# Running sums in one early transfer, zeros on TensorE, and quarters of the first expert layer ahead of time

## The chip, the cores and the metric

The kernel runs on one core of a Trainium2 chip. Its five engines each work through a queue of their own: TensorE (PE; its weight loads are PEld) multiplies, VectorE (DVE) and ScalarE (ACT) work element by element and read the products, GpSimd (POOL) helps on data outside the product buffers, and SyncE (SP) issues transfers. The metric is the device time of one execution in microseconds (us).

## What is computed

Attention with a running-sum bias, then a dense mixture of four experts, then a two-layer network with squared relu, all in float32:

```python
scores = scale * np.matmul(q, k.transpose(0, 1, 3, 2))      # q, k: (2, 8, 576, 64)
cum = np.cumsum(np.maximum(s, 0.0), axis=-1)                # s: (2, 8, 576)
bias = -(cum[:, :, :, None] - cum[:, :, None, :])
scores = np.where(causal, -1e9, scores + np.minimum(bias, 0.0))
attn = softmax(scores)                                      # denominator + 1e-9
x = (attn @ v) as rows of 512                               # 1152 rows
p = domain_probs / (domain_probs.sum(-1, keepdims=True) + 1e-09)
out = sum over e of p[:, e:e+1] * (np.maximum(x @ w1[e], 0) @ w2[e])   # 512 -> 1024 -> 512
r = np.maximum(out @ w_in, 0)                               # 512 -> 2048
return (r * r) @ w_out
```

## The kernel before, in words

Every exact product is made of float32r parts: an operand is split into a rounded high part and the rest (`less`, line 76), and three products (high by high, high by low, low by high) are summed in a product buffer.

**Steps.** Attention runs as a pipeline over steps, one step for one tile of queries of one head (loop at line 683). Steps 0 to 15 are batch 0, queries 0 to 255, eight heads with two tiles each, two heads to a loaded group. Steps 16 to 39 are batch 0, queries 256 to 575, eight heads with three tiles. From step 40 on comes batch 1. In iteration n, step n gets its scores on TensorE (`do_qk`, line 415), step n-1 its masked scores and row minimum on VectorE (`do_scores`, the reduction, line 459), step n-2 its exponentials on ScalarE (`do_exp`, line 473), step n-3 its sums and scaling (VectorE, lines 485 and 486, and GpSimd, line 489), step n-4 its transposes on TensorE (line 512), and step n-5 their copy out (line 536). Two heads' attention times v (`do_pv`, line 560) gives a 128-row slice of x, which `do_x` (line 577) splits into `xh` and `xl`.

**Running sums.** The raw s is loaded eight times into 128 rows (`sc`, line 590), made positive and scaled on VectorE (line 593), and summed by a scan (line 594). For steps 0 to 15 the sums enter the scores as matmuls with a one-hot operand `pick` (line 610, made from `one`, line 608, a copy of parts of the identity), with the parts `cum_k` and its negation `cum_q`. For all later steps the sums of all 576 columns, split in two parts (`aug`, lines 626 to 628), are written to memory (`aug_d`, line 630) and read back as rows of the operands `th` and `tl`, whose other rows come from q and k. All this stands ahead of the loop in the code; so do the loads of the first four groups' q and k (`raw_p`, line 323) and of the expert shares (`praw`, line 623). `p_norm` (line 632) turns `praw` into shares with four VectorE operations at n = 12 in the code.

**Weights.** The first expert's sixteen weight pieces are loaded (`w_load`, line 91, three buffers) and split (`w_split`, ScalarE line 114 and VectorE line 78) at the steps of `SPLIT_AT`: the eight of the first layer at steps 0 to 14, the eight of the second at 22 to 36.

**Fill.** The first expert's work on tokens 0 to 255 is cut into parts (`fill_of`, line 663): eight column blocks of the first layer (`first`: 12 matmuls of 256 columns, line 196, over four 128-row slices of x, each from one pair of heads), then the second layer (`second`, line 222). They are issued between steps 21 and 45 at an even rate of columns per step (`X_AT`, line 31), those of tokens 256 to 511 after step 45. The experts that follow (lines 763 to 1111) have an order of their own.

**Order.** SyncE's queue keeps the order of the code. The other engines' order is made by a scheduler that goes by modelled times; `issue_after` puts instructions behind a given one on its engine, `pin` and `manual_schedule` keep the code's order.

Of the kernel before, what the change touches and what calls it, by code (L numbers as in the profile page):

```python
# [16 lines left out]
P = 128  # L17
# [11 lines left out]
SPLIT_AT = [*range(0, 16, 2), *range(22, 38, 2)]  # L29
NP = 5  # L30
X_AT = 21, 45
KMAX = 512

# [13 lines left out]
def fused_kernel(ctx, tc, qk, v, s, dp, w1, w2, wi, wo, out):  # L47
# [17 lines left out]
    make_identity(nc, ident)  # L65
# [4 lines left out]
    aug_d = dram.tile([2, B * H, 2, S], F32, name="aug_d")  # L70
# [119 lines left out]
    def l1_pe(e, c, f):  # L190
        t0, n = c
        ps = ph_tile()
        i = 0
        for kk in range(KD):
            for wh, x in ((0, xh), (0, xl), (1, xh)):
                nc.tensor.matmul(  # L196
                    ps[:, :n],
                    lhsT=w1_ap(e, wh, kk, f),
                    rhs=x[:, kk, t0 : t0 + n],
                    start=(i == 0),  # L200
                    stop=(i == 3 * KD - 1),
                )
                i += 1
        return ps
# [95 lines left out]
    with tc.tile_pool(name="att", bufs=2) as att, tc.tile_pool(name="atc", bufs=1) as const_a:  # L300
# [15 lines left out]
        st_pools[:] = [att, WBUF, "raw_w"]
# [18 lines left out]
        def bc_load(g):  # L335
            if g.plain:
                return
            r0 = g.b * H + g.heads[0]
            nc.sync.dma_start(out=g.th[AQ, : g.nq].bitcast(F32), in_=aug_d[0, r0, :, g.q0 : g.q1])
            nc.sync.dma_start(out=g.tl[AK, S : S + g.nk].bitcast(F32), in_=aug_d[1, r0, :, : g.nk])  # L340

        def part(name):
            tiles = [const_a.tile([P, 2 * S], F32R, name=f"{name}{i}") for i in range(2)]
            for t in tiles:
                c, ones = (slice(0, S), AK) if name == "th" else (slice(S, 2 * S), AQ)
                nc.gpsimd.memset(t[:64, c].bitcast(F32), 0.0)
                nc.gpsimd.memset(t[ones, c].bitcast(F32), 1.0)
            return tiles

        th_tiles, tl_tiles = part("th"), part("tl")  # L350
        for i, g in enumerate(groups):
            g.th, g.tl = th_tiles[i % 2], tl_tiles[i % 2]
# [62 lines left out]
        def do_qk(t):  # L415
            u, g = t.u, t.u.group
            if g.plain:
# [9 lines left out]
                one = pick[rows, u.h // 2, :]  # L427
                sums = ((one[:, : t.n], cum_k[rows, : t.w]), (cum_q[rows, t.q0 : t.q0 + t.n], one[:, : t.w]))
                for i, (lhs, rhs) in enumerate(sums):
                    nc.tensor.matmul(ps[: t.n, : t.w], lhsT=lhs, rhs=rhs, start=False, stop=(i == 1))  # L430
# [18 lines left out]
        def do_scores(t):  # L449
# [22 lines left out]
        def do_exp(t):  # L472
            nc.scalar.activation(  # L473
# [130 lines left out]
        pick = wt[0, 2, 3][:, 0, :].rearrange("p (h n) -> p h n", n=256)  # L604
# [4 lines left out]
        for a, z in ((0, 1), (1, 4)):  # L609
            nc.scalar.copy(pick[:, a:z, :], one[:, a:z].unsqueeze(2).to_broadcast([P, z - a, 256]))  # L610
        sums_to(P, 0, 256, 0.0)
        cum_k = att.tile([P, 256], F32R, tag="cum_k", name="cum_k", bufs=1)
        cum_q = att.tile([P, 256], F32R, tag="cum_q", name="cum_q", bufs=1)
        nc.scalar.copy(cum_k, cum[:, :256])
        for r0 in (32, 96):
            rows = slice(r0, r0 + 32)
            less(nc.vector, cum_k[rows], cum[rows, :256], cum_k[rows])
        nc.vector.tensor_scalar(cum_q, cum_k.bitcast(F32), -1.0, None, op0=ALU.mult)
        sums_to(B * H, 256, S, cum[: B * H, 255:256])
        cum = cum[: B * H, :]  # L620
        augs = [att.tile([B * H, 2, S], F32R, tag="ptk", name="aug", bufs=3) for _ in range(2)]
# [41 lines left out]
        def fill_of(c):  # L663
            tiles = range(c[0] // P, (c[0] + c[1]) // P)

            def first(f):
                l1_evac(0, c, f, l1_pe(0, c, f))
# [6 lines left out]
            parts = [(lambda f=f: first(f), 12 * c[1]) for f in range(NF)]  # L674
            return parts + [(lambda t=t, f=f: second(t, f), 3 * DM) for t in tiles for f in range(NF)]

# [6 lines left out]
        for n in range(nsteps + 8):  # L683
# [476 lines left out]
```

## Time and profile before

| | us |
|---|---|
| median of 3 runs | 718.39 (718.21 to 718.71) |
| the profiled execution | 719.2 |
| its span, first to last instruction | 717.4 |
| busy: TensorE, VectorE, ScalarE, GpSimd | 689.6, 507.6, 353.1, 311.9 |
| TensorE busy in the first 10 us, the next 10 | 2.15, 7.75 |

"Busy" counts the time in which an engine has at least one instruction under way; a matmul's end is modelled, so a TensorE that is marked busy need not run at its peak. A timeline row tells when an instruction began, how long it took, its engine, line, operation and tile, and in brackets how long the engine had been idle and for whom it waited. On SyncE a row is the issue of a transfer, not the transfer.

### The profile page before, as it was taken

What the parts mean: (1) busy time and instruction counts of PE and PEld (TensorE: products, weight loads), DVE (VectorE), ACT (ScalarE), POOL (GpSimd) and SP (SyncE); (2) the same over time, 40 slices, a digit from 0 to 9 for tenths busy, and PEclk for the clock granted to TensorE, in tenths of its full rate; (3) what the DMA queues carried; (4) which work ended last, traced back from release to release, by engine and by line L of the source; (5) the groups of instructions that cost most, each with busy time, mean ns of one, the idle gap of its engine ahead of it and who ended that gap; (6) DMA issues with size and microseconds to landing.
All of it is one profiled execution on the core that took longest, in us unless ns stands there. A gap on an engine that the chain in (4) does not pass through costs nothing.

```text
span 717.4 us, 11852 instructions
## 1 busy us (share of the span) xinstructions
PE 689.6 (96%) x4100; PEld 598.5 (83%) x4100; DVE 507.6 (71%) x1145; ACT 353.1 (49%) x881; POOL 311.9 (43%) x332
## 2 busy tenths in 40 slices
PE   4999999999999999999999999999999999999997
PEld 3678788778998998989989989889997888899996
DVE  6668667762378548787787787869587788955463
ACT  4789767752254453443342534335474445535341
POOL 4446534431043675292580852822528625704000
PEclk9999999999999999999999999999999999999999
DMA  4554333200121234344242443441203232210012
GB/s 139 169 162 148 93 85 84 62 25 1 60 84 64 89 114 136 108 136 139 85 165 90 148 147 105 132 121 70 60 22 111 77 122 96 89 30 1 1 59 73
DMA packets 37179, 66.37 MB, mean 93 GB/s; under 512 B 4512, under 2 KB 12208, under 8 KB 37120
## 3 DMA queue, kind: packets, MB, share of 16 engines
q1 hardware_dynamic: 27904, 40.45, 18.7%
q10 hardware_dynamic: 9216, 25.17, 10.7%
q8 instruction: 32, 0.52, 0.3%
q14 instruction: 27, 0.22, 0.1%
HBM read 52.87 MB, written 10.90 MB: 89 GB/s over the span
## 4 chain that ended last, share of the span: by engine, by line
PE 74%; DVE 12%; ACT 4%; issue 4%; DMA 2%; POOL 2%; SPq 1%; ACTq 0%; DVEq 0%; POOLq 0%
PE y L953 26%; PE ph L935 17%; PE pc L935 7%; PE ph L196 7%; PE y L222 6%; PE o L560 4%; PE pt L512 3%; DVE dy L144 2%; PE s L439 2%; DVE raw_d L148 2%; PE s L440 1%; DVE raw_d L140 1%; ACT p L473 1%; POOL w L78 1%; DVE h L988 1%
## 5 line engine op out<-in xcount | busy, mean ns | idle before, releaser
L953 PE MATMUL y<-w,h 128*128 128x512 f32 x1080 | 276.7, 393 | 0.7 <-ACT h L993 0.7
L953 PEld LDWEIGHTS y<-w,h 128*128 128x128 f32 x1080 | 194.2, 188 | 32.0 <-ACT h L993 0.9
L935 PE MATMUL ph<-tx,w 128*128 128x256 f32 (+1 forms) x720 | 116.2, 297 | 0.1
L935 PEld LDWEIGHTS ph<-tx,w 128*128 128x128 f32 x720 | 106.9, 190 | 7.6 <-ACT u L976 0.9
L976 ACT COPY u<-ph 128x256 f32<-128x256 f32 (+1 forms) x120 | 47.7, 397 | 96.1 <-PE ph L935 93.9
L78 POOL TENSOR_TENSOR w<-raw_w,w 128x512 fp32r<-128x512 f32 x58 | 79.4, 1383 | 21.5 <-ACT w L902 21.5
L935 PE MATMUL pc<-xh,w 128*128 128x256 f32 (+1 forms) x320 | 78.2, 299 | 6.2 <-DVE r L992 2.8
L935 PE MATMUL ph<-xh,w 128*128 128x256 f32 (+1 forms) x320 | 78.3, 299 | 1.7 <-DVE h L988 1.2
L489 POOL TENSOR_SCALAR p<-p,stat 128x128 f32<-128x128 f32 (+8 forms) x80 | 46.8, 597 | 72.8 <-DVE stat L486 30.4
L78 POOL TENSOR_TENSOR w<-val,w 128x512 fp32r<-128x512 f32 x40 | 58.6, 1480 | 43.4 <-PE ph L196 41.7
L133 POOL TENSOR_SCALAR dy<-dy 128x512 f32<-128x512 f32 x32 | 20.0, 626 | 116.1 <-ACT dy L131 108.7
L935 PEld LDWEIGHTS pc<-xh,w 128*128 128x128 f32 x320 | 55.9, 188 | 10.4 <-DVE h L988 3.8
L935 PEld LDWEIGHTS ph<-xh,w 128*128 128x128 f32 x320 | 56.1, 189 | 5.1 <-DVE h L988 1.9
L473 ACT ACTIVATE p<-p,stat 128x128 f32<-128x128 f32 (+8 forms) x80 | 46.6, 583 | 23.7 <-DVE stat L459 20.3
L222 PE MATMUL y<-w,h 128*128 128x512 f32 x216 | 57.7, 396 | 0.0
L196 PE MATMUL ph<-xh,w 128*128 128x256 f32 (+1 forms) x256 | 57.3, 299 | 0.1
L459 DVE CUSTOM_DVE_ANT_0 p<-s,mask 128x128 f32<-128x128 f32 (+8 forms) x80 | 35.8, 451 | 17.7 <-PE pt L512 8.8
L935 PE MATMUL ph<-xl,w 128*128 128x256 f32 (+1 forms) x160 | 47.5, 297 | 0.0
L935 PE MATMUL pc<-xl,w 128*128 128x256 f32 (+1 forms) x160 | 47.3, 296 | 0.0
L994 DVE TENSOR_TENSOR h<-r,h 128x256 fp32r<-128x256 f32 (+1 forms) x64 | 36.2, 571 | 13.7 <-ACT h L993 12.5
L196 PEld LDWEIGHTS ph<-xh,w 128*128 128x128 f32 x256 | 43.1, 188 | 1.5 <-DVE h L210 0.4
L222 PEld LDWEIGHTS y<-w,h 128*128 128x128 f32 x216 | 38.7, 188 | 6.2 <-DVE stat L459 0.3
(135 smaller groups left out, 1272.7 us busy)
## 6 DMA issues: line engine op xcount, KB each, us to landing
raw_w<-in_w SPq DMA_DIRECT2D x64, 256.0 KB
raw_d<-in_wi ACTq DMA_DIRECT2D x16, 512.0 KB
staged<-dy ACTq DMA_DIRECT2D x32, 256.0 KB
raw_d<-in_wo ACTq DMA_DIRECT2D x16, 512.0 KB
raw_w<-staged SPq DMA_DIRECT2D x32, 256.0 KB
raw<-in_qk SPq DMA_DIRECT2D x40, 144.0 KB
v<-in_v SPq DMA_DIRECT2D x8, 256.0 KB
out<-acc_a SPq DMA_DIRECT2D x6, 256.0 KB
```

The source lines that it names most:

```text
L78: eng.tensor_tensor(out_, a, b.bitcast(F32), op=ALU.subtract)
L196: nc.tensor.matmul(ps[:, :n], lhsT=w1_ap(e, wh, kk, f), rhs=x[:, kk, t0 : t0 + n], start=(i == 0), stop=(i == 3 * KD - 1),)
L222: mm = nc.tensor.matmul(ps, lhsT=h[:, hh, o : o + P], rhs=w2_ap(e, wh, f), start=(f == 0 and i == 0), stop=(f == NF - 1 and i == 2),)
L459: nc.vector.tensor_tensor_reduce(t.p[: t.n, a:z], ps[: t.n, : z - a], t.bias[:, a:z], scale=-0.125, scalar=init, op0=ALU.add, op1=ALU.min, ...
L473: nc.scalar.activation(t.p[: t.n, : t.w], t.p[: t.n, : t.w], AF.Exp, bias=t.nmax, scale=-1.0, accum_out=t.st[: t.n, 4 + t.c : 5 + t.c],)
L489: nc.gpsimd.tensor_scalar(t.p[: t.n, : t.w], t.p[: t.n, : t.w], t.st[: t.n, 6 + t.c : 7 + t.c], 1.0, op0=ALU.mult, op1=ALU.mult)
L512: nc.tensor.transpose(tp_ap(t, j), t.p[: t.n, kt[j] : kt[j + 1]], ident[: t.n, : t.n])
L560: return nc.tensor.matmul(u.o[i * D : (i + 1) * D, qs - u.q0 : u.nq], lhsT=vv[:kn, j, i * D : (i + 1) * D], rhs=rhs, start=(j == 0), stop= ...
L935: nc.tensor.matmul(ps[:, :n], lhsT=pw[q][s][:, wh, c : c + P], rhs=x_part(b, xn, xx, k2), start=(first and m == 0), stop=(m == 5), skip_gr ...
L953: nc.tensor.matmul(ps, lhsT=hs[j][:, hh, o : o + P], rhs=wt[e, 2, g][:, wh, j * DM : (j + 1) * DM], start=(g % 2 == 0 and i == 0 and j == ...
L976: nc.scalar.copy(t[:, :n], ps[:, :n])
L994: nc.vector.tensor_tensor(lo, r, hi.bitcast(F32), op=ALU.subtract)
```

## The change

- s comes in one transfer of its first 256 columns into all 128 rows, issued first, and one of the other 320 columns into 16 rows. Relu and factor are made on ScalarE. The high and low parts of the sums are made by a cast and one operation with a per-row factor `is_low` into `less_cum`; there are two one-hot operands, plus and minus, in place of a negated sum.
- The sums of columns 256 to 575, their split and their write (once, not twice with the sign turned) move to step 4 (`AUG_AT`, `later_sums`). The sign goes into the constant rows of `tl`.
- `p_norm`, the later sums and the weight splits get places behind step n-1's reduction; the splits also behind step n-2's exponentials. The first-layer splits start at step 2, not 0.
- TensorE multiplies a tile of zeros by itself: nine matmuls of 512 columns at the start, and one behind the scores of each of the steps 0 to 8.
- For tokens 0 to 255 and column blocks 0 to 3, the first layer's products of a 128-row slice of x are issued one quarter per step after that slice's pair of heads is done (pairs 0 to 2), into two product buffers that hold two blocks each; what is left in the fill for these blocks is the last slice.

```diff
-SPLIT_AT = [*range(0, 16, 2), *range(22, 38, 2)]
+SPLIT_AT = [*range(2, 17, 2), *range(22, 38, 2)]
+WARM = 9, 1, 9
+AUG_AT = 4
...
-    def l1_pe(e, c, f):
+    def l1_pe(e, c, f, ps=None, kks=range(KD), start=True):
         t0, n = c
-        ps = ph_tile()
-        i = 0
-        for kk in range(KD):
+        ps = ph_tile() if ps is None else ps
+        i = 3 * kks[0]
+        for kk in kks:
...
+        zeros = const_a.tile([P, 512], F32R, name="zeros")
+        nc.vector.memset(zeros.bitcast(F32), 0.0)
+
+        def keep_warm(after, n):
+            with tc.issue_after(after) if after is not None else nullcontext():
+                for _ in range(n):
+                    nc.tensor.matmul(idle, lhsT=zeros[:, :P], rhs=zeros, start=True, stop=True)
+
+        idle = ph_tile()
+        keep_warm(None, WARM[0])
...
-        for r0 in range(0, P, B * H):
-            nc.sync.dma_start(out=sc[r0 : r0 + B * H, :], in_=s)
+        nc.sync.dma_start(
+            out=sc[:, :256],
+            in_=s[:, :256].unsqueeze(0).to_broadcast([P // (B * H), B * H, 256]),
+        )
...
-            nc.vector.tensor_scalar(sc[:rows, c0:c1], sc[:rows, c0:c1], 0.0, 8.0, op0=ALU.max, op1=ALU.mult)
+            nc.scalar.activation(sc[:rows, c0:c1], sc[:rows, c0:c1], AF.Relu, scale=8.0)
...
+                nc.sync.dma_start(out=sc[: B * H, 256:], in_=s[:, 256:])
...
+        def pick(i, a, z):
+            src = one[:, a:z].unsqueeze(2).to_broadcast([P, z - a, 256])
+            nc.scalar.activation(picks[i][:, a:z, :], src, AF.Copy, scale=1.0 - 2.0 * i)
...
+        nc.vector.tensor_copy(high, cum[:, :256])
+        nc.vector.scalar_tensor_tensor(
+            less_cum, high.bitcast(F32), is_low, cum[:, :256], op0=ALU.mult, op1=ALU.subtract
+        )
...
+        def later_sums():
+            sums_to(B * H, 256, S, cum[: B * H, 255:256])
+            parts = att.tile([B * H, 2, S], F32R, tag="raw", name="aug", bufs=3)
+            total = cum[: B * H, :]
+            nc.scalar.copy(parts[:, 0, :], total)
+            less(nc.vector, parts[:, 1, :], total, parts[:, 0, :])
+            nc.sync.dma_start(out=aug_d, in_=parts.bitcast(F32))
...
             def first(f):
-                l1_evac(0, c, f, l1_pe(0, c, f))
+                if c[0] == 0 and f < 4:
+                    l1_evac(0, c, f, l1_pe(0, c, f, halves[f], range(KD - 1, KD)))
+                else:
+                    l1_evac(0, c, f, l1_pe(0, c, f))
...
+        def begin(kk):
+            if kk == 0:
+                for f in (0, 2):
+                    ps = ph_tile()
+                    halves[f], halves[f + 1] = ps[:, :256], ps[:, 256:]
+            early.extend(lambda f=f: quarter(kk, f) for f in range(4))
...
                 do_qk(cur)
+                if n < WARM[2]:
+                    keep_warm(cur.mm.ins, WARM[1])
+                if early:
+                    with tc.issue_after(cur.mm.ins):
+                        early.pop(0)()
...
             if n in SPLIT_AT:
-                w_step()
+                with tc.issue_after(s1.red.ins), tc.issue_after(s2.exp.ins):
+                    w_step()
+            if n == AUG_AT:
+                with tc.issue_after(s1.red.ins):
+                    later_sums()
             if n == 12:
-                p_norm()
+                with tc.issue_after(s1.red.ins):
+                    p_norm()
```

TensorE's queue at the program's start held the scores of steps 0 to 2 (raw_p is q and k, cum_k and cum_q the running sums):

```order
L420 MATMUL s<-raw_p 128x128
L420 MATMUL s<-raw_p 128x256
L420 MATMUL s<-raw_p 128x128
L430 MATMUL s<-cum_k,w 128x128
L430 MATMUL s<-cum_k,w 128x256
L430 MATMUL s<-cum_k,w 128x128
```

In the changed program it begins with the zeros (L332), and one more follows each step's sums (less_cum):

```order
L332 MATMUL ph<-zeros 128x512 x9
L436 MATMUL s<-raw_p 128x128
L436 MATMUL s<-raw_p 128x256
L436 MATMUL s<-raw_p 128x128
L449 MATMUL s<-less_cum,w 128x128
L449 MATMUL s<-w,less_cum 128x128
L332 MATMUL ph<-zeros 128x512
L449 MATMUL s<-less_cum,w 128x256
L449 MATMUL s<-w,less_cum 128x256
L332 MATMUL ph<-zeros 128x512
```

The scores of q and k keep their place, and the zeros have come in ahead of and between them.

VectorE's queue from the first scan to step 2's reduction held, before, the sums of all columns, their parts, and the first operation of `p_norm` (L634); L459 is the reduction:

```order
L594 SCALAR_TENSOR_TENSOR cum<-sc 128x256
L594 SCALAR_TENSOR_TENSOR cum<-sc,cum 16x320
L78 TENSOR_TENSOR cum_k<-cum,cum_k 32x256 x2
L618 TENSOR_SCALAR cum_q<-cum_k 128x256
L78 TENSOR_TENSOR aug<-cum,aug 16x576
L628 TENSOR_SCALAR aug<-aug 16x1152
L634 TENSOR_REDUCE psum__364<-praw 128x9
L459 ISA p,stat<-s,mask 128x128
L459 ISA stat 128x1
L635 TENSOR_SCALAR psum__364<-psum__364 128x9
L459 ISA p,stat<-s,mask 128x256
```

In the changed program the same stretch (L478 is the reduction, L79 the subtract of a weight split):

```order
L615 SCALAR_TENSOR_TENSOR cum<-sc 128x256
L644 CAST cum_hi<-cum 128x256
L646 SCALAR_TENSOR_TENSOR less_cum<-cum_hi,is_low,cum 128x256
L478 ISA p,stat<-s,mask 128x128
L478 ISA stat 128x1
L478 ISA p,stat<-s,mask 128x256
L478 ISA stat 128x1
L79 TENSOR_TENSOR w<-raw_w,w 128x512
L478 ISA p,stat<-s,mask 128x128
```

The later columns, their parts and `p_norm` have left the place ahead of step 0's reduction, and a weight split stands between the reductions of steps 1 and 2.

TensorE's queue after the first attention-times-v product (o) held only scores and transposes (pt) before:

```order
L560 MATMUL o<-ptk,v 64x256 x2
L560 MATMUL o<-ptk,v 64x128 x2
L512 MATMUL pt<-ident,p 128x128 x2
L420 MATMUL s<-raw_p 128x256
L430 MATMUL s<-cum_k,w 128x256
L430 MATMUL s<-w,cum_q 128x256
```

In the changed program, some rows behind that product, the quarters of the first layer (L199, xh and xl the parts of x) come in:

```order
L531 MATMUL pt<-ident,p 128x128
L199 MATMUL ph<-xh,w 128x256 x2
L436 MATMUL s<-raw_p 128x256
L449 MATMUL s<-less_cum,w 128x256
L449 MATMUL s<-w,less_cum 128x256
L531 MATMUL pt<-ident,p 128x128 x2
L199 MATMUL ph<-xl,w 128x256
L199 MATMUL ph<-xh,w 128x256 x2
L199 MATMUL ph<-xl,w 128x256
```

Matmuls of the first layer stand among the two-head steps now; before, the first of them stood behind the scores of step 20.

## Rows read from the trace of the kernel before

**Rows 1.** The page: busy time, share and count; TensorE in 40 slices.

```profile
PE 689.6 (96%) x4100; PEld 598.5 (83%) x4100; DVE 507.6 (71%) x1145; ACT 353.1 (49%) x881; POOL 311.9 (43%) x332
...
PE   4999999999999999999999999999999999999997
```

**Rows 2.** Windows: stretch, length, engines' busy us (instructions), granted clock, DMA share, GB/s.

```profile
12.93:36.75 23.82, 21.88 (x87) 15.34 (x88) 16.43 (x59) 17.74 (x59) 10.68 (x16) 1.00 0.55 167
36.75:46.66 9.91, 8.74 (x46) 5.79 (x45) 7.22 (x24) 7.81 (x21) 4.26 (x6) 1.00 0.49 143
46.66:96.00 49.34, 49.34 (x351) 39.94 (x349) 34.82 (x117) 39.12 (x98) 27.35 (x30) 1.00 0.46 134
```

**Rows 3.** Timeline of SyncE's queue: start, duration, line, transfer.

```profile
0.72 3.64 SPq L590 DMA_DIRECT2D sc<-in_s  x8
4.41 0.68 SPq L323 DMA_DIRECT2D raw_p<-in_qk  x1
...
7.69 0.60 SPq L623 DMA_DIRECT2D praw<-in_dp  x1
11.02 0.79 SPq L630 DMA_DIRECT2D aug_d<-aug  x2
```

**Rows 4.** Timeline of all engines, 0 to 13 us.

```profile
2.06 0.28 POOL masks.py:199 TENSOR_SCALAR_AFFINE_SELECT ident<-ident 128x128 f32<-128x128 f32 x1
...
3.48 1.96 DVE L608 COPY one<-ident 32x4 f32<-32x4 f32 x4
...
6.72 0.69 DVE L594 TENSOR_TENSOR_SCAN cum<-sc 128x256 f32<-128x256 f32 x1
...
7.85 1.65 PE L420 MATMUL s<-raw_p 64*128 64x128 f32 x6 [7.85 <-DMA raw_p<-in_qk]
...
9.26 0.29 DVE L618 TENSOR_SCALAR cum_q<-cum_k 128x256 fp32r<-128x256 f32 x1
...
9.61 0.78 PE L430 MATMUL s<-w,cum_q 64*128 64x128 f32 x3
...
12.17 0.19 DVE L634 TENSOR_REDUCE psum__364<-praw 128x9 f32<-128x36 f32 x1 [1.18 <-DMA praw<-in_dp]
12.30 0.29 DVE L459 CUSTOM_DVE_ANT_0 p<-s,mask 128x128 f32<-128x128 f32 x1
...
12.93 0.28 DVE L459 CUSTOM_DVE_ANT_0 p<-s,mask 128x128 f32<-128x128 f32 x1
```

**Rows 5.** Timeline of TensorE, at 37, 44 and 52 us.

```profile
37.07 0.63 PE L439 MATMUL s<-th,tl 128*128 128x512 f32 x1
37.50 0.63 PE L440 MATMUL s<-tl,th 128*128 128x512 f32 x1
...
44.28 0.39 PE L439 MATMUL s<-th,tl 128*128 128x512 f32 x1
44.51 0.40 PE L440 MATMUL s<-tl,th 128*128 128x512 f32 x1
...
52.49 0.40 PE L196 MATMUL ph<-xh,w 128*128 128x256 f32 x2
...
52.84 0.40 PE L196 MATMUL ph<-xh,w 128*128 128x256 f32 x2
```

**Rows 6.** The windows view of 46.6 to 66 us, columns as in rows 2.

```profile
46.60:66.00 19.40, 19.40 (x154) 16.94 (x153) 15.34 (x52) 16.94 (x44) 12.46 (x13) 1.00 0.56 165
```

**Rows 7.** Groups by form, 0 to 20 us: busy, mean ns, idle before.

```profile
L346 POOL MEMSET th<- 64x576 f32 x2 | 1.1, 572 | 0.0
...
L78 DVE TENSOR_TENSOR w<-raw_w,w 128x512 fp32r<-128x512 f32 x4 | 2.9, 740 | 1.1 <-ACT w L114 1.0
...
L114 ACT CAST w<-raw_w 128x512 fp32r<-128x512 f32 x4 | 2.3, 610 | 0.1
...
L626 ACT CAST aug<-cum 16x576 fp32r<-16x576 f32 x1 | 0.7, 671 | 0.5 <-DVE cum L594 0.5
```

**Rows 8.** Waits, 12 to 100 us: total, times, longest.

```profile
ACT w L114 <- DMA raw_w<-in_w: 2.6, 3, 1.3
```

More of the change, by code (lines that the diff above doesn't have):

```diff
@@ L199, in l1_pe @@
                     rhs=x[:, kk, t0 : t0 + n],
-                    start=(i == 0),
+                    start=(i == 0 and start),
                     stop=(i == 3 * KD - 1),
+                    skip_group_check=True,
                 )
+                if i == 0:
+                    l1_first[0] = mm
                 i += 1
@@ L346, in part @@
                 nc.gpsimd.memset(t[:64, c].bitcast(F32), 0.0)
-                nc.gpsimd.memset(t[ones, c].bitcast(F32), 1.0)
+                nc.gpsimd.memset(t[ones, c].bitcast(F32), 1.0 if name == "th" else -1.0)
             return tiles
-        th_tiles, tl_tiles = part("th"), part("tl")
-        for i, g in enumerate(groups):
-            g.th, g.tl = th_tiles[i % 2], tl_tiles[i % 2]
         def qk_split(g):
@@ L426, in do_qk @@
                 )
-                one = pick[rows, u.h // 2, :]
-                sums = ((one[:, : t.n], cum_k[rows, : t.w]), (cum_q[rows, t.q0 : t.q0 + t.n], one[:, : t.w]))
+                plus, minus = (x[rows, u.h // 2, :] for x in picks)
+                sums = (
+                    (minus[:, : t.n], less_cum[rows, : t.w]),
+                    (less_cum[rows, t.q0 : t.q0 + t.n], plus[:, : t.w]),
+                )
                 for i, (lhs, rhs) in enumerate(sums):
-                    nc.tensor.matmul(ps[: t.n, : t.w], lhsT=lhs, rhs=rhs, start=False, stop=(i == 1))
+                    t.mm = nc.tensor.matmul(ps[: t.n, : t.w], lhsT=lhs, rhs=rhs, start=False, stop=(i == 1))
                 t.ps = [(ps, 0, t.w)]
@@ L472, in do_exp @@
         def do_exp(t):
-            nc.scalar.activation(
+            t.exp = nc.scalar.activation(
                 t.p[: t.n, : t.w],
@@ L618, in fused_kernel @@
[L618 to L621, printed above, removed]
+        def pick(i, a, z):
+            src = one[:, a:z].unsqueeze(2).to_broadcast([P, z - a, 256])
+            nc.scalar.activation(picks[i][:, a:z, :], src, AF.Copy, scale=1.0 - 2.0 * i)
+        pick(0, 0, 1)
+        pick(1, 0, 1)
@@ new lines, in fused_kernel @@
+        sums_to(P, 0, 256, 0.0)
+        high = att.tile([P, 256], F32R, tag="cum_hi", name="cum_hi", bufs=1)
+        less_cum = att.tile([P, 256], F32R, tag="less_cum", name="less_cum", bufs=1)
+        nc.vector.tensor_copy(high, cum[:, :256])
+        nc.vector.scalar_tensor_tensor(
+            less_cum, high.bitcast(F32), is_low, cum[:, :256], op0=ALU.mult, op1=ALU.subtract
+        )
+        pick(0, 1, 4)
+        pick(1, 1, 4)
+        th_tiles, tl_tiles = part("th"), part("tl")
+        for i, g in enumerate(groups):
+            g.th, g.tl = th_tiles[i % 2], tl_tiles[i % 2]
@@ L672, in second, with quarter @@
                     y_evac(0, t)
-            parts = [(lambda f=f: first(f), 12 * c[1]) for f in range(NF)]
+            parts = [(lambda f=f: first(f), (3 if c[0] == 0 and f < 4 else 12) * c[1]) for f in range(NF)]
             return parts + [(lambda t=t, f=f: second(t, f), 3 * DM) for t in tiles for f in range(NF)]
+        early = []
+        halves = {}
+        def begin(kk):
[4 more added lines that the diff above has]
+            early.extend(lambda f=f: quarter(kk, f) for f in range(4))
+        def quarter(kk, f):
+            with tc.issue_after(l1_first[0].ins) if kk == 0 and f % 2 else nullcontext():
+                l1_pe(0, (0, 256), f, halves[f], range(kk, kk + 1), start=f % 2 == 0)
         fill, rate, owed = [], 0, 0
@@ L727, in fused_kernel @@
                 do_x(x_next)
+                if x_next.b == 0 and x_next.q0 == 0 and x_next.h < 6:
+                    begin(x_next.h // 2)
             x_next = None
```

53 lines of the change are left out of this document (22 added, 31 removed).

## The prediction

> **What bounds the kernel now.** I read the page's busy shares and slices first [rows 1]. TensorE is busy for 96% of the span, and of its slices only the first and the last are under 9 tenths. So whatever the change is worth lies early, or in TensorE work that leaves the dense part. The order of the changed program says the same: on every engine its rows equal the old ones again from the first half of batch 1 onward (on TensorE, the last 3337 of some 3970). What stands behind that point, near 100 us, moves as a block, and the question is only how much earlier the block starts.
>
> So I cut the first 96 us into four stretches: up to step 0's score reduction, and then [rows 2] from step 2's to about step 16's (the two-head steps, 23.82 us), to where the fill begins (9.91 us), and on into batch 1 (49.34 us). TensorE is marked busy in 21.88 us of the second, 8.74 of the third and all of the fourth.
>
> The first stretch is a chain of queues. SyncE issues eight copies of s in turn, from 0.72 to 4.36 us, and only then the first head pair's q and k (raw_p, at 4.41) [rows 3]; TensorE waits for it until 7.85 [rows 4]. The last operand of the scores is made at 9.55 (9.26 + 0.29) and its matmuls issue from 9.61. Yet step 0's reduction stands behind a reduction of praw on VectorE's queue, and praw was issued at 7.69 and waited for until 12.17. So step 0 is reduced at 12.30, step 2 at 12.93.
>
> In the second and third stretch TensorE looks full, but at half speed. [...] TensorE is thus the limit of the sixteen steps (about 1.7 us each: 23.82 over 14), and ScalarE, busy in 17.74 of 23.82 us (0.74), is next. Where the clock is high, from 46.6 to 66.0, ScalarE is busy for 16.94 of 19.40 us, or 0.87 [rows 6]. I take 0.87 as what ScalarE reaches beside a fast TensorE.
>
> **Part 1: start of the steps.** One copy of s replaces eight. With the 0.46 us pitch of those issues, raw_p is issued at 0.72 + 0.46 = 1.18 and, with the 3.44 us that it takes now (4.41 to 7.85), lands at 4.6. The sums wait for something else: the `one` copies stand ahead of the scan on VectorE and need the identity. On GpSimd three clears now stand ahead of its select where two did, so it starts at 2.06 + 0.57 and ends at 2.9 [rows 4, 7]. Then 1.96 (copies), 0.69 (scan), and a cast and a subtract of 128x256 (the nearest row is the negation, 0.29; I take 0.35 each) [rows 4]: the operand is there at 6.3, and with 0.8 for its matmuls, as at 9.61 now, the reduction comes at about 7.2, with praw no longer ahead of it. The new copy of s has until 4.9 to land, unseen. That is 5.1 us earlier for step 0. The small new clears on VectorE fall before 2.9, where it waits for the identity anyway; the four pick copies run on ScalarE beside the scan.
>
> Not all of it lasts. At step 2 the weight split is placed right behind step 1's reduction on VectorE, ahead of step 2's. It needs the first weight piece. Its issue comes after two of s (0.46 each), the five of raw_p and v (3.28, from 4.41 to 7.69) and praw (0.65 with its pitch): 0.72 + 0.92 + 3.28 + 0.65 = 5.6 [rows 3]. From issue to landing I bound it by raw_p's 3.44 and praw's 4.48 (7.69 to 12.17), both behind other transfers: 9.0 to 10.1. Then 0.61 of cast and 0.74 of subtract [rows 7]: step 2 is reduced between 10.4 and 11.4. [...]
>
> **Part 2: steps 2 to 20.** Nine zero matmuls of 512 columns from about 1.3 us take 9 x 0.43 = 3.9 us at the lower level, to 5.2, before raw_p can be used: they delay nothing by more than 0.6 us. If they lift the clock, the sixteen steps are no longer TensorE's: halving 21.88 us gives about 11, plus zeros (some 5 x 0.22 behind step 2) and 24 to 36 quarter matmuls at 0.118 (below), about 16 us. ScalarE sets the pace: 17.74 plus the later sums' relu and cast (at most 0.67 each, by the old cast of 16x576 [rows 7]), 19.0; over 0.87, 21.8 against 23.82: **2.0 us**. The bounds are 0.95 (20.0, so 3.8) and the present 0.745 (25.5, so a loss of 1.7). Third stretch: 7.81 over 0.87 is 9.0 against 9.91, **0.9 us** (1.7 at 0.95; nothing, if what it waits for there stays as late). The later sums are written at step 4 and read at step 12; at over 1 us per step nothing waits for them.
>
> **Part 3: quarters.** 36 of the 96 first-layer matmuls of tokens 0 to 255 (3 of 4 contraction slices, 4 of 8 column blocks, 3 products) leave steps 21 to 45 for steps 10 to 21, where TensorE then has room. Three such matmuls take 0.35 us (52.49 to 52.84 [rows 5]), so 36 take 4.2 us out of the 49.34. ScalarE is at 39.12 of 49.34 there; in 45.1 us it would be at 0.87, just the level that it holds now in 46.6 to 66. So all 4.2 can come, but with nothing to spare, and the last second-layer product now reaches its weights in the very step that splits them (step 36: 15360 first-layer columns and 7 x 1536 of the second stand ahead of it, at 1664 a step 15.7 steps after step 21). I take **3.5 us**, bounds 0 and 4.2.
>
> **Sum.** 2.1 + 2.0 + 0.9 + 3.5 = 8.5 us. The profiled execution took 719.2 (span 717.4 and 1.8 around it), so 710.7; the median of the runs shown, 718.39, lies 0.8 below that execution, so **709.9**.
>
> [...]
>
> **Rivals.** (a) More comes: the piece lands early and ScalarE reaches 0.95: 3.1 + 3.8 + 1.7 + 4.2 = 12.8, so 705.6. For it: of some 6 us in which ScalarE idles in the second stretch, its waits for weights come to 2.6 [rows 8], and the rest is the chain that the slow clock stretches. Against: no stretch of the trace holds 0.95. (b) The steps stay tied to transfers and to the chain of score, exp, sum, scale: ScalarE stays at its present share, part 2 gives -1.7 and 0, part 3 half of its 4.2, so 2.1 - 1.7 + 2 = 2.4 and 716.0. For it: ScalarE waits for weight pieces three times even now [rows 8]. Against: those loads stand behind the write of the sums at 11.02, which waits for VectorE, and that is gone. (c) **Slower.** TensorE has nothing to multiply between the scores of the first five steps, done near 8.5, and step 2's reduction at 10.8; the clock falls there, and the zeros and quarters then cost double without lifting it: 5 zeros x 0.43 = 2.1, 36 quarters x 0.21 = 7.7 on a TensorE that is the limit of steps 2 to 20. Then -2.1 + 2.1 + 7.7 - 3.5 = +4.2, so 722.6. It decides from the point where the first 512-column zero after 8.5 us is followed at 0.43 us again and stays so until step 20. For it: now the lower level lasts through the sixteen steps in spite of a TensorE that is marked busy all along. Against: between 37.5 and 44.28 us the clock rises, and what TensorE did before that were matmuls over all 128 rows [rows 5]; zeros and quarters are of that kind, the scores of the sixteen steps (64 rows, [rows 4]) aren't.
>
> **Numbers.** Forecast (707.5 to 712.5) 0.56; (a) 0.14; (b), with all between 712.5 and 717, 0.20; (c) 0.08; 0.02 beyond. A measurement of this kernel tells about 0.2% (1.4 us) from no change, so faster means under 716.95. Of (b), 0.04 lies within 0.2%, and of (c) 0.02. Faster 0.87, same 0.06, slower 0.07. The range reaches below (a) and above (b): 704.5 to 716.5, leaving out (c) and the edges.
>
> **What would show it.** Step 0's reduction near 7 us and step 2's near 10.8, with the subtract of the first weight piece right ahead of it; matmuls of 512 columns 0.22 us apart by then; step 16's scores some 4 us earlier than now, the fill's first matmul 5; ScalarE at about 0.87 from step 2 on. The forecast is wrong if the zeros behind step 2 start 0.43 us apart, if ScalarE waits for raw_w at each split, or if TensorE shows idle time in steps 21 to 45, where the 4.2 us were taken out.

## The result, and the profile after

The changed kernel takes 724.55 us (median of 4 runs, 723.3 to 726.87), the kernel before beside it 718.55: a ratio of 1.008 [1.0056, 1.0104]. It is slower by 6.0 us, where 8.5 us of gain were forecast, and near the 722.6 of rival (c). The profiled execution took 723.3 us (span 721.5). Medians and ratios leave out executions over 1.5% longer than the same kernel's fastest: one of no_quarters below (845.87 us), one of the kernel before beside it (843.74), and four of held_all's six, which took 732 to 740 us at mean granted clocks of 0.964 to 0.975.

The page after, lines as in [rows 1], with the granted clock of the 40 slices:

```profile
PE 700.9 (97%) x4118; PEld 604.2 (84%) x4118; DVE 504.8 (70%) x1146; ACT 354.8 (49%) x884; POOL 310.4 (43%) x332
...
PE   9989999999999999999999999999998999999997
...
PEclk7598999999999999999999999999999999999999
```

TensorE is busy for 11.3 us more, and its granted clock is now below full in three of the first four slices. Windows cut at the reductions of steps 2, 16, 20 and 40 (columns as in [rows 2]), first of after:

```profile
11.52:40.60 29.08, 28.53 (x111) 20.45 (x112) 16.97 (x62) 17.24 (x55) 10.11 (x18) 0.61 0.33 101
40.60:48.06 7.46, 7.35 (x52) 5.33 (x52) 4.79 (x17) 5.92 (x16) 3.92 (x5) 1.00 0.71 214
48.06:95.03 46.97, 44.07 (x286) 33.98 (x285) 35.48 (x112) 37.79 (x92) 24.84 (x27) 0.93 0.42 125
```

The same three of before:

```profile
12.93:37.42 24.49, 22.55 (x89) 15.99 (x90) 16.43 (x59) 17.97 (x60) 10.68 (x16) 1.00 0.56 168
37.42:45.14 7.72, 6.55 (x31) 3.93 (x29) 6.09 (x19) 6.10 (x16) 3.42 (x5) 1.00 0.50 148
45.14:89.69 44.55, 44.55 (x325) 36.15 (x325) 33.77 (x115) 37.45 (x92) 26.89 (x29) 1.00 0.45 131
```

Step 2 comes 1.4 us sooner, steps 2 to 16 take 4.6 us longer, 16 to 20 are 0.3 shorter, and 20 to 40, though TensorE has less to do there (286 matmuls, not 325), 2.4 longer: together 5.3, and step 79 is 5.1 us late. So the loss lies in two stretches.

**The first.** Timeline of TensorE after (start, duration):

```profile
1.48 4.21 PE L332 MATMUL ph<-zeros 128*128 128x512 f32 x9 [1.48 <-DVE zeros L325]
...
7.67 0.49 PE L332 MATMUL ph<-zeros 128*128 128x512 f32 x1
8.09 0.38 PE L449 MATMUL s<-less_cum,w 64*128 64x256 f32 x1
...
10.61 0.79 PE L332 MATMUL ph<-zeros 128*128 128x512 f32 x1
11.34 0.79 PE L436 MATMUL s<-raw_p 64*128 64x128 f32 x2
...
12.38 0.79 PE L332 MATMUL ph<-zeros 128*128 128x512 f32 x1
13.10 1.22 PE L436 MATMUL s<-raw_p 64*128 64x256 f32 x2
```

The zeros did lift the clock: at 7.67 a zero takes 0.49 us, and what stands behind it starts after 0.42. At 10.61 and 12.38 it takes 0.79, and the next starts after 0.72 to 0.73. Windows around that moment:

```profile
5.60:10.60 5.00, 4.93 (x20) 3.04 (x19) 2.21 (x8) 3.38 (x8) 1.46 (x2) 1.00 0.89 292
10.60:34.40 23.80, 23.70 (x79) 16.86 (x78) 13.13 (x46) 13.34 (x42) 6.58 (x11) 0.50 0.34 103
```

The granted clock is 0.50 for 23.8 us, and it fell with TensorE marked busy in 4.93 of the 5 us ahead. So a zero behind each step's scores didn't hold it. VectorE's and SyncE's queues show two waits that the prediction didn't have:

```profile
7.90 0.29 DVE L478 CUSTOM_DVE_ANT_0 p<-s,mask 128x128 f32<-128x128 f32 x1 [0.72 <-PE s L449]
...
10.91 0.69 DVE L79 TENSOR_TENSOR w<-raw_w,w 128x512 fp32r<-128x512 f32 x1 [1.85 <-ACT w L115]
11.52 0.28 DVE L478 CUSTOM_DVE_ANT_0 p<-s,mask 128x128 f32<-128x128 f32 x1
...
15.72 0.42 DVE L478 CUSTOM_DVE_ANT_0 p<-s,mask 128x256 f32<-128x256 f32 x1 [3.63 <-PE pt L531]
```

```profile
5.97 5.99 SPq L92 DMA_DIRECT2D raw_w<-in_w  x4
12.00 0.43 SPq L400 DMA_DIRECT2D v<-in_v  x1
19.05 0.33 SPq L663 DMA_DIRECT2D aug_d<-aug  x1
19.48 0.37 SPq L92 DMA_DIRECT2D raw_w<-in_w  x1
19.90 0.53 SPq L351 DMA_DIRECT2D raw<-in_qk  x1
```

Step 3's reduction waits 3.63 us for the transposes (pt) of step 0: `sc` and `cum` hold two of the five buffers of tag p until the later sums are made, so step 3 needs the first one back. And SyncE issues nothing from 12.43 to 19.05, where the write of the later sums waits for them; a weight piece and the next q and k stand behind it.

**The second.** Timeline of TensorE after:

```profile
52.65 0.29 PE L459 MATMUL s<-tl,th 128*64 128x288 f32 x1
54.75 0.42 PE L199 MATMUL ph<-xh,w 128*128 128x256 f32 x1 [1.81 <-DVE h L216]
...
56.46 0.79 PE L531 MATMUL pt<-ident,p 64*128 64x64 f32 x5 [0.86 <-POOL p L508]
...
57.99 0.63 PE L458 MATMUL s<-th,tl 128*128 128x512 f32 x1
58.42 0.63 PE L459 MATMUL s<-tl,th 128*128 128x512 f32 x1
```

With the quarters gone from here, TensorE comes to block 1's last slice while VectorE still reads block 0, which shares its product buffer: 1.81 us. After it and a wait of 0.86 us for GpSimd's scaling, 512 columns take 0.43 us again, where before they took 0.23 [rows 5].

### The profile page after: what moved, and what is told of

The parts are those of the page before. It is cut to its first block, busy times and chain, and to the rows that moved or that the text cites. A ratio compares the mean times of both kernels' runs of the same rounds, so it can differ in the third digit from the quotient of the medians.

```text
span 721.5 us, 11873 instructions
## 1 busy us (share of the span) xinstructions
PE 700.9 (97%) x4118; PEld 604.2 (84%) x4118; DVE 504.8 (70%) x1146; ACT 354.8 (49%) x884; POOL 310.4 (43%) x332
## 4 chain that ended last, share of the span: by engine, by line
PE 78%; DVE 11%; ACT 4%; issue 3%; POOL 2%; DMA 0%; ACTq 0%; DVEq 0%; POOLq 0%; SPq 0%
PE y L1017 26%; PE ph L999 17%; PE pc L999 7%; PE ph L199 7%; PE y L228 6%; PE o L579 4%; PE pt L531 4%; DVE dy L145 2%; PE s L458 2%; PE s L436 2%; DVE raw_d L149 2%; PE s L459 1%; PE ph L332 1%; DVE raw_d L141 1%; POOL w L79 1%
## 5 line engine op out<-in xcount | busy, mean ns | idle before, releaser
L79 POOL TENSOR_TENSOR w<-raw_w,w 128x512 fp32r<-128x512 f32 x58 | 79.5, 1385 | 20.6 <-ACT w L966 20.6
L999 PE MATMUL ph<-xh,w 128*128 128x256 f32 (+1 forms) x320 | 78.0, 298 | 1.3 <-DVE h L1052 0.8
L79 POOL TENSOR_TENSOR w<-val,w 128x512 fp32r<-128x512 f32 x40 | 58.6, 1480 | 43.3 <-ACT w L959 43.3
L199 PE MATMUL ph<-xh,w 128*128 128x256 f32 (+1 forms) x256 | 60.5, 308 | 1.9 <-DVE h L216 1.8
L492 ACT ACTIVATE p<-p,stat 128x128 f32<-128x128 f32 (+8 forms) x80 | 46.6, 582 | 18.4 <-DVE stat L478 14.2
L478 DVE CUSTOM_DVE_ANT_0 p<-s,mask 128x128 f32<-128x128 f32 (+8 forms) x80 | 35.8, 452 | 27.8 <-PE pt L531 16.4
L199 PEld LDWEIGHTS ph<-xh,w 128*128 128x128 f32 x256 | 44.6, 194 | 4.2 <-DVE h L216 2.5
```

Source lines behind the costliest of these rows:

```text
L79: eng.tensor_tensor(out_, a, b.bitcast(F32), op=ALU.subtract)
L199: mm = nc.tensor.matmul(ps[:, :n], lhsT=w1_ap(e, wh, kk, f), rhs=x[:, kk, t0 : t0 + n], start=(i == 0 and start), stop=(i == 3 * KD - 1), ...
L478: t.red = nc.vector.tensor_tensor_reduce(t.p[: t.n, a:z], ps[: t.n, : z - a], t.bias[:, a:z], scale=-0.125, scalar=init, op0=ALU.add, op1= ...
L492: t.exp = nc.scalar.activation(t.p[: t.n, : t.w], t.p[: t.n, : t.w], AF.Exp, bias=t.nmax, scale=-1.0, accum_out=t.st[: t.n, 4 + t.c : 5 + ...
L999: nc.tensor.matmul(ps[:, :n], lhsT=pw[q][s][:, wh, c : c + P], rhs=x_part(b, xn, xx, k2), start=(first and m == 0), stop=(m == 5), skip_gr ...
```

## The experiments

The profile behind each row is one execution; "step" is that reduction's start against the kernel before's profile, in us. Medians of before beside the sets were 717.83 to 719.96, so the ratio decides.

| kernel | median us | ratio to before | step 2 | 16 | 40 | 79 |
|---|---|---|---|---|---|---|
| after | 724.55 | 1.008 [1.0056, 1.0104] | -1.4 | +3.2 | +5.3 | +5.1 |
| own_tiles | 724.37 | 1.0086 [1.0063, 1.011] | -1.8 | +5.5 | +7.7 | +7.4 |
| no_zeros | 719.03 | 1.0007 [0.9984, 1.003] | -4.0 | -0.3 | +2.0 | +1.8 |
| no_quarters | 723.09 | 1.0066 [1.0041, 1.0091] | -1.4 | +4.6 | +4.2 | +4.2 |
| zeros_held | 726.83 | 1.0111 [1.0071, 1.0152] | -1.6 | +6.5 | +8.0 | +9.7 |
| own_noz | 721.36 | 1.0024 [1.0006, 1.0042] | -4.0 | +0.6 | +2.1 | +1.9 |
| noz_pairs | 720.01 | 1.0018 [0.999, 1.0045] | -4.0 | -2.5 | +0.1 | -0.4 |
| noz_aug | 719.14 | 1.0001 [0.9982, 1.0019] | -4.0 | -3.8 | -0.7 | -1.1 |
| all4 | 720.05 | 1.0013 [0.9994, 1.0031] | -4.0 | -1.4 | +0.8 | +0.3 |
| start_alone | 718.95 | 1.0008 [0.9985, 1.003] | -4.0 | -3.5 | -1.0 | 0.0 |
| start_own | 719.05 | 1.0007 [0.9982, 1.0032] | -4.0 | -3.7 | -2.0 | -0.6 |
| quarters_twice | 720.38 | 1.0029 [0.9998, 1.0059] | -4.0 | -1.1 | +0.7 | +0.6 |
| held_all | 718.57 | 0.9999 [0.9961, 1.0038] | -1.2 | -1.3 | +1.3 | +1.4 |
| late_warm | 718.49 | 0.9984 [0.9966, 1.0003] | -4.0 | -2.8 | -2.0 | -1.3 |
| late_warm_own | 720.45 | 1.0005 [0.999, 1.0019] | -4.0 | -1.6 | -1.2 | +1.0 |
| before_warm | 721.98 | 1.0029 [1.0013, 1.0044] | -0.3 | +0.6 | +0.9 | +1.8 |
| late_few | 717.01 | 0.9964 [0.9949, 0.998] | -4.0 | -3.5 | -2.0 | -1.1 |
| late_mid | 715.68 | 0.9956 [0.994, 0.9972] | -4.0 | -4.0 | -2.2 | +0.4 |

**First set: one part of the change each.** own_tiles (the p buffers):

```diff
-        sc = att.tile([P, S], F32, tag="p", name="sc", bufs=NP)
-        cum = att.tile([P, S], F32, tag="p", name="cum", bufs=NP)
+        sums = att.tile([P, 1280], F32, tag="ptk", name="sums", bufs=3)
+        sc = sums[:, :S]
+        cum = sums[:, S : 2 * S]
```

> The changed kernel (724.55 us), but the running sums sc and cum lie in one tile of the ptk ring instead of two of the five p tiles, so that a step's p tile need not wait for the transposes of three steps before. Theory A (buffers): in the changed kernel step 3's reduction waits at 15.72 for step 0's transposes, 3.6 us; with five p tiles free it comes near 12.5 and some 4 us last to the end: 720.5. Theory B (clock): TensorE at the lower clock from 10.7 to 34 us is the limit anyway, the gain at step 3 is gone again by step 10: 723.5 to 725. Either way the granted clock still falls near 10.7.

Step 3 came at 11.59 instead of 15.72, but the median didn't move. The wait is real, and taking it away alone gains nothing.

no_zeros:

```diff
-WARM = 9, 1, 9
+WARM = 0, 0, 0
```

> The changed kernel without any zero matmul. Theory B (clock): the zeros do not hold the clock beyond 10.7 us and the six behind that cost 0.43 us each on a TensorE that is the limit: 2.6 us less, 722.0, though the first scores then run at the lower clock. Rival C: the zeros are harmless and keep the clock up for the first scores, so that without them the start is later: 724.5 to 726. Theory A expects no change of the wait at step 3.

5.5 us come back, where 2.6 were expected: nearly the whole loss goes with the zeros. But the edit also changes VectorE's order, which the scheduler makes. Step 2's reduction now stands ahead of the first weight subtract, and in the changed kernel (rows above) behind it:

```profile
8.91 0.29 DVE L478 CUSTOM_DVE_ANT_0 p<-s,mask 128x128 f32<-128x128 f32 x1
...
10.59 0.73 DVE L79 TENSOR_TENSOR w<-raw_w,w 128x512 fp32r<-128x512 f32 x1 [0.56 <-ACT w L115]
```

No run separates this order from the zeros; that own_tiles gained nothing from 4.1 us at step 3 speaks against a large share. And not one of the 4 us by which step 2 is sooner reaches the end.

no_quarters (blocks 0 to 3 whole in the fill; the diff in part):

```diff
...
-                if x_next.b == 0 and x_next.q0 == 0 and x_next.h < 6:
+                if False:
```

> The changed kernel with the first expert's first layer whole in the fill, as before the change (no quarters); zeros and early sums stay. Theory B: twelve quarters at the lower clock (0.21 each) no longer cost 2.5 us before 34 us, and TensorE has enough to do in steps 21 to 45 so that the second fall of the clock near 53.5 us goes, worth 3 to 4 us; the 4.2 us of work come back: 722 to 723. Rival D: the quarters save their 4.2 us and have no part in the loss: 728.5.

Steps 16 to 40 take 51.9 us (before 52.3, after 54.4): the lag at step 16 isn't added to. Early quarters bought nothing in the stretch that they left; the zeros' loss stays.

zeros_held (zeros in 16 steps, four each):

```diff
-WARM = 9, 1, 9
+WARM = 9, 4, 16
```

> The changed kernel with four zero matmuls behind the scores of each of the steps 0 to 15, not one behind those of 0 to 8. If it is too little work of this kind that lets the clock fall at 10.7 us, it stays high through the sixteen steps; a step then costs TensorE some 0.8 + 4 x 0.22 = 1.7 us, no more than before: 717 to 722, and the wait for the p tiles is what is left of the loss. If the clock falls all the same, 27 + 28 more zeros at 0.43 us cost over 20 us: 745.

Its window where after had 0.50, and two of its waits (5 to 45 us):

```profile
10.60:34.40 23.80, 23.43 (x113) 16.46 (x113) 11.19 (x41) 11.76 (x38) 6.39 (x11) 1.00 0.36 102
```

```profile
DVE p L478 <- PE pt L531: 10.0, 3, 4.1
ACT th L378 <- DMA raw<-in_qk: 5.8, 2, 4.3
```

The clock is held, and the ratio is the highest of all. ScalarE is busy for 0.49 of the stretch, not 0.87: TensorE works off zeros, and the buffers and the loads behind SyncE's wait are as late as in the changed kernel (step 3's reduction at 15.73, the write at 19.16).

**Second set: without zeros, one wait each.** noz_aug issues the write from another queue, noz_pairs multiplies both blocks of a product buffer before either is read, own_noz and all4 (all of them) add the buffers of own_tiles (the diff in part):

```diff
-            nc.sync.dma_start(out=aug_d, in_=parts.bitcast(F32))
+            nc.scalar.dma_start(out=aug_d, in_=parts.bitcast(F32))
...
-                    l1_evac(0, c, f, l1_pe(0, c, f, halves[f], range(KD - 1, KD)))
+                    if f % 2 == 0:
+                        ps = [l1_pe(0, c, i, halves[i], range(KD - 1, KD)) for i in (f, f + 1)]
+                        for i in (f, f + 1):
+                            l1_evac(0, c, i, ps[i - f])
```

> Without zeros (719.03 us before this edit), and the sums in a tile of the ptk ring. Without zeros step 3's reduction came at 11.99, so the p tiles hold it less: theory A now expects 1 us at most at step 3 and 718 to 719; theory B (clock) the same or no change, since the clock is low throughout the sixteen steps either way.

> Without zeros, and the last slices of two column blocks that share a product buffer are both multiplied before either is taken out. [...]

> Without zeros, and the write of the later sums is issued on ScalarE's queue, not SyncE's. Theory F (queue): SyncE waits 3.1 us for the sums at step 4 and again 10 us on the value loads, so q and k of the three-tile steps come late (ScalarE waits 1.6 us for raw); with the write elsewhere the loads start 3 us earlier and steps 12 to 16, where 5.7 of 6.0 us of gain are lost, keep 1 to 2 us: 717 to 718. Rival: those steps lose their gain to twelve quarters at the lower clock (2.5 us) and to the value loads, and the time stays at 719.

> The three edits together, without zeros: sums in the ptk ring, pairs multiplied before they are taken out, the sums' write on ScalarE's queue. If the waits found are the whole loss, the gains add: 712 to 715. If the low clock of the first 36 us is the limit, only the pairs' part shows: 714 to 716.

No ratio fell below 1. The gains expected of own_noz and all4 didn't come, and noz_aug stayed where its rival had it. No run shows the pairs' gain that all4's ranges count in: noz_pairs has a ratio of 1.0018, no_zeros 1.0007. The waits moved on: noz_pairs has none on `h` (1.82 us in no_zeros), and in its place this one on GpSimd's scaling:

```profile
51.30 0.79 PE L531 MATMUL pt<-ident,p 64*128 64x64 f32 x5 [3.78 <-POOL p L508]
```

**Third set: what is the start worth alone?** start_alone is no_zeros, no_quarters and noz_aug in one, start_own adds own_tiles; held_all is the change with two zeros in each of 16 steps, own_tiles and noz_aug's write; quarters_twice is noz_aug with (in part)

```diff
-                    l1_evac(0, c, f, l1_pe(0, c, f, halves[f], range(KD - 1, KD)))
+                    l1_evac(0, c, f, l1_pe(0, c, f, halves[f], range(KD), start=f % 2 == 0))
```

> Leaves out the zeros and puts the expert's first layer back whole into the dense part (all four slices of every block from step 21 on), and issues the write of the sums on ScalarE's DMA queue, so that SyncE's loads do not stand behind it. What is left of the change is the early transfer and the later sums. Theory 1 (the quarters, taken out of the dense part, leave TensorE waiting there, and its clock falls again): steps 16 to 40 take about 52 us as in the kernel before, the 3.8 us that noz_aug was ahead at step 16 are still there at step 40 and at step 79, and the time is 714.5 to 716. Theory 2 (the early start is lost in the dense part whatever is in it, since VectorE and ScalarE set the pace there): step 40 is less than 1 us ahead of the kernel before and the time is 718 to 719.5.

> As start_alone, and the scores and the running sums of the first step stand in a tile of their own ring instead of two of the five that the steps' products use. If the five tiles hold up steps 3 to 8, step 3 comes 3 to 4 us earlier than in start_alone and the time is 713 to 715; if ScalarE and the low clock set the pace by step 8 (as own_tiles and own_noz showed), the two are equal within 1 us.

> Leaves out the zeros, the write of the sums on ScalarE's queue, as in noz_aug, and multiplies the 36 quarters twice: early, as the change does, and again whole in the dense part, where they start the products afresh, so that the early ones are of no use. TensorE thus has 36 products of 256 columns (4.2 us at 0.118 us each) more to do than in noz_aug. Theory 1 (without them TensorE waits in steps 21 to 40 and its clock falls, which costs more than they took): steps 16 to 40 take about 52 us instead of 55.4, no second fall of the clock between 45 and 60 us, and the time is 715 to 717.5, below noz_aug's 719.14 although more is multiplied. Theory 2 (the work of the dense part is what it takes): the added products lengthen it by 2 to 4.2 us, and the time is 721 to 723.

> The change with the waits taken away that the zeros_held run met: two zeros behind each of 16 steps (one behind nine in the change), scores and sums of the first step in a tile of their own, the write of the sums on ScalarE's queue. The forecast's reason (a held clock lets ScalarE set the pace at 0.87 us a step): granted clock 1.00 from 7 to 45 us, step 16 reached at 33 us or before (37.42 in the kernel before), time 712 to 716. The rival (the zeros themselves stand in TensorE's order ahead of the next step's work, and cost as much as the clock gives): step 16 at 37 us or later, time 719 to 724.

Theory 1 of start_alone fell: no quarter is moved, and the start still goes. So did that of quarters_twice: work put back didn't pay, and its 720.38 lies between the two ranges. start_own has step 3 at 10.18, 1.8 us sooner than start_alone, and the same time. held_all, freed of the waits and with a granted clock of 1.00 from 7 to 45 us in its profile, takes 24.3 us from step 2 to 16, not the forecast's 21.8. What start_alone's profile shows ahead of the dense part is this (timeline of TensorE, then a window):

```profile
36.65 0.30 PE L459 MATMUL s<-tl,th 128*64 128x288 f32 x1
36.78 0.27 PE L531 MATMUL pt<-ident,p 128*128 128x128 f32 x1
37.85 0.41 PE L531 MATMUL pt<-ident,p 128*128 128x128 f32 x2 [0.80 <-ACT ptk L555]
39.19 0.75 PE L531 MATMUL pt<-ident,p 128*128 128x128 f32 x3 [0.93 <-POOL p L508]
...
40.81 0.63 PE L458 MATMUL s<-th,tl 128*128 128x512 f32 x1
41.23 0.63 PE L459 MATMUL s<-tl,th 128*128 128x512 f32 x1
```

```profile
39.00:43.00 4.00, 3.72 (x15) 2.44 (x17) 2.31 (x8) 2.51 (x8) 3.17 (x4) 0.57 0.68 193
```

The clock had just risen (288 columns in 0.13 us at 36.65); after two waits it is low again until 43 us (512 columns in 0.42 us at 40.81), and the dense part begins with it.

**Fourth and fifth set: zeros there, and not at the start.** late_warm is start_alone with 16 zeros over these waits, late_warm_own adds own_tiles, before_warm is the kernel before with the same zeros; late_few and late_mid have eight. The diff of late_warm, in part:

```diff
...
-                if n < WARM[2]:
-                    keep_warm(cur.mm.ins, WARM[1])
+                if 15 <= n <= 20:
+                    keep_warm(cur.mm.ins, 6 if n == 15 else 2)
```

late_mid has 3 and 1 in place of 6 and 2, late_few 2, 4 and 2 behind steps 18, 19 and 20.

> start_alone with 16 zeros later: six behind the scores of step 15 (where TensorE waited 1.41 us) and two behind those of each of steps 16 to 20 (where it waited 0.80 and 0.93 us and its clock, just risen at 36.5 us, fell again until 43 us). If the start's gain is lost because the clock is low again when the dense part begins: granted clock high from 36 us on, step 24 at 48.5 us or before (49.4 in start_alone, 51.86 in the kernel before), step 40 at 86.5 to 87.5 us and the time 715 to 717. If the dense part takes back any start by waits of its own: step 40 within 1 us of the kernel before's 89.69 us and the time 718 to 719.5.

> late_warm, and the scores and running sums of the first step in a tile of their own. Expected within 0.7 us of late_warm by both theories; by the first 714.5 to 717, by the second 718 to 719.5.

> The kernel before with the same 16 zeros at steps 15 to 20 and nothing else changed. Its clock was high from 43.5 us, before its dense part begins at 46.6 us, and granted 1.00 through steps 20 to 40, so by the first theory the zeros have little to lift: the time is 717.5 to 719.5 and late_warm beats it by 2 to 3 us. By the second theory the two kernels are equal within 1 us. If this one is the faster, the zeros and not the start are what the dense part lacks.

> late_warm with 8 of its 16 zeros, where TensorE waits once its clock has risen: two behind the scores of step 18, four behind step 19, two behind step 20, none sooner. late_warm's zeros cost 0.8 us at step 16 (2.75 us ahead there, 3.53 in start_alone). If they are needed only over the two waits at 37 to 39 us, step 16 is 3.5 us ahead, step 28 is 4 us ahead or more, and the time is 0.5 to 1 us below late_warm's, 716.5 to 718. If the clock falls in spite of them, or was not what late_warm gained by, the time is start_alone's, 718.5 to 719.5.

> late_warm with half as many zeros at the same places: three behind the scores of step 15, one behind those of each of steps 16 to 20. Between start_alone and late_warm: 717 to 719, nearer the first if one zero a step does not hold the clock over the waits of 0.80 and 0.93 us, as one a step did not hold it at 10.7 us in the change.

Windows of late_warm:

```profile
36.00:50.00 14.00, 12.70 (x91) 10.03 (x89) 9.42 (x35) 11.83 (x31) 8.38 (x10) 1.00 0.54 159
50.00:60.00 10.00, 10.00 (x79) 8.35 (x79) 9.41 (x31) 9.85 (x26) 6.74 (x7) 1.00 0.56 161
```

The clock stays at 1.00, and step 28 is 4.3 us ahead (0.9 in start_alone). Not all of that is the clock: from 50 to 60 us start_alone's reads 1.00 too, but its TensorE is busy for 9.06 of the 10 us and waits once for VectorE, 0.94 us. late_warm's median lies in the second theory's range, its lead at step 40 (2.0 us) nearer the first's. With equal zeros, the start is worth 3.5 us: 718.49 against 721.98 of before_warm (2.8 us by the means). The sixteen zeros alone make the kernel before slower, by 0.29% [0.13, 0.44].

With half as many, late_mid and late_few beat the kernel before by 0.44% [0.28, 0.60] and 0.36% [0.20, 0.51]: versions faster than both kernels. The kernel before with eight zeros wasn't run, so how much of this is the start's isn't shown. The time goes with the mean granted clock of an execution: late_few's nine executions at 0.999 or 1.000 took 716.52 to 717.63, its three at 0.997 or 0.998 took 718.63 to 718.85; start_alone's six have 0.993 to 0.998.

late_mid's profile is of its slowest execution (718.35; the other five took 715.24 to 716.01), and there the clock was 0.66 from 40 to 45 us, so its marks in the table don't stand for the median. late_few came within its range, though step 28 is 2.5 us ahead and not the 4 expected; late_mid came 1.3 us below its own. late_warm_own lies 1 us above the range of either theory; the buffers of own_tiles gain nothing here either.

## Why the prediction was wrong

- **Part 1 held** at its own place: step 0 at 7.90 (predicted 7.2), step 2 at 11.52 behind the first weight subtract at 10.91 (predicted 10.8): 1.4 us of the 2.1. It said nothing of step 3, whose p tile was now held by the sums. No run shows the sum's 2.1 us or rival (a)'s 3.1 with that subtract ahead of step 2's reduction: the changed kernels with the early zeros have 1.2 to 1.8, those without them 4.0 in VectorE's other order. The first piece was issued at 5.97 and cast from 10.26, when ScalarE had waited for it.
- **Part 2 is the step that failed**: "If they lift the clock, the sixteen steps are no longer TensorE's". They lifted it and didn't hold it: 29.08 us from step 2 to 16 where before had 24.49 and 21.8 were forecast for a like stretch. Nor was the rest of the step right: with the clock held, ScalarE was busy for only 0.49 of the time (zeros_held), and with the waits taken away as well, steps 2 to 16 took 24.3 us (held_all). "At over 1 us per step nothing waits for them" looked at who reads the later sums, not at what stands behind their write on SyncE. The argument against rival (b), that loads no longer wait behind that write, overlooked the same.
- **Part 3 failed in its sign**: 3.5 us of gain became 2.4 us of loss from step 20 to 40. "Nothing to spare" was the warning, but it watched ScalarE's 0.87: TensorE ran into VectorE (1.81 us) and GpSimd (0.86), and behind these waits 512 columns took 0.43 us again. In no_quarters the loss is gone, 51.9 us from step 16 to 40. But start_alone, whose dense part is as whole, takes 54.8 there and quarters_twice 54.0. So work that is taken out is not the only way to lose there; an earlier start alone loses too.
- **Rival (c)** had the side and almost the time, by a mechanism half right. There was no gap of TensorE ahead of the fall (busy in 4.93 of the 5 us); and its price of a zero, 0.43 us, was the pitch of 512-column scores [rows 5], where a single zero between other products took 0.59 to 0.72. The six from 10.61 on took 4.1 us, of the 5.5 that no_zeros gave back; the rest isn't accounted for. Its argument against itself, that zeros are of the kind that lifts the clock, was right for nine in a row and wrong for one a step; held_all's two a step held it (granted 1.00 from 7 to 45 us).
- **What the start is worth** came out as 3.5 us, above the 2.1 of part 1, but only with the clock held at the start of the dense part and without the early zeros.

Behind the dense part start_alone loses another 1.2 us between steps 63 and 65. TensorE's transposes there wait for GpSimd's scaling in both kernels, and start at the same time. The kernel before, then start_alone:

```profile
129.33 0.62 PE L512 MATMUL pt<-ident,p 128*64 128x128 f32 x4 [0.65 <-POOL p L489]
...
129.36 0.63 PE L531 MATMUL pt<-ident,p 128*64 128x128 f32 x4 [1.74 <-POOL p L508]
```

So what stands behind 100 us does not move as a block, as the prediction had it. By the traces, the shapes on TensorE are the old ones only from 124.9 us of the kernel before on.

Open: how much of noz_aug's lead at step 16 is the queue (below); what VectorE's changed order costs beside the zeros; and whether early quarters could pay beside late zeros, which wasn't tried (they hold the buffers that the zeros write).

## What to carry to other kernels

Try filler work on TensorE in its idle time just ahead of dense work, in small amounts. Here nine zeros at the start and one per step cost 5.5 us, together with the order that came with them, and didn't hold the clock (0.50 from 10.60 us); with eight over the waits before the dense part, the early start came out 0.36 and 0.44% ahead. Before work is taken out of a full stretch, ask which engine is next there and whether TensorE would then wait. And list what stands behind a moved transfer on its queue, not only who reads its data.

## What the runs showed of the hardware

The clock can rise at different moments under the same instructions. noz_aug and quarters_twice have the same instructions on TensorE up to the fill (step 21), and at 28.3 us they are within 0.01 us of each other. noz_aug:

```profile
28.30 0.41 PE L199 MATMUL ph<-xh,w 128*128 128x256 f32 x1
28.65 0.48 PE L436 MATMUL s<-raw_p 64*128 64x128 f32 x2
...
29.24 0.87 PE L579 MATMUL o<-ptk,v 128*64 128x256 f32 x8
30.04 0.44 PE L531 MATMUL pt<-ident,p 128*128 128x128 f32 x2
```

quarters_twice:

```profile
28.31 0.42 PE L199 MATMUL ph<-xh,w 128*128 128x256 f32 x1
28.66 0.79 PE L436 MATMUL s<-raw_p 64*128 64x128 f32 x2
...
29.70 1.55 PE L579 MATMUL o<-ptk,v 128*64 128x256 f32 x8
31.18 0.69 PE L531 MATMUL pt<-ident,p 128*128 128x128 f32 x2
```

In the one the eight products take 0.87 us, in the other 1.55, and by step 16 they are 2.8 us apart. The executions of one kernel spread by some 5 us here (716.76 to 721.7 in 27 of before); differences of 1 to 3 us between single profiles prove nothing, and several rows of the table differ by no more.

quarters_twice has its rise behind 37.06, where 512 columns still take 0.43 us, noz_aug at 28.65. In the changed kernel one rise stands behind the nine zeros that begin at 1.48 us (a zero takes 0.49 us at 7.67), and one fall behind 1.81 us of waiting at 54.75 (512 columns in 0.43 us at 57.99). The fall at 10.61 (a zero takes 0.79 us), with TensorE marked busy, does not come from an idle stretch that any row shows.

The granted clock does not show every low stretch. quarters_twice's reads 1.00 from 30 to 40 us, with the 0.43 us at 37.06 in it. The kernel before's reads 1.00 in every stretch of [rows 2]; the half speed in the first two shows in the spacing, 0.43 us at 37.07 against 0.23 at 44.28 [rows 5], and in eight products of attention times v, 1.55 us at 23.52 against 0.87 at 45.10.
